# Another order for the first loads, sums on ScalarE for the first scales, and a planner that counts eight transfers in flight

## The chip, the cores and the metric

One core of a Trainium2 chip runs the kernel. The time is the device time of one execution in microseconds (us). The time before is 1918.88 us, the median of three runs (1918.65 to 1921.34).

## What is computed

Attention in chunks, then a mixture of eight experts whose weights are balanced over the tokens. For 4 batches of 768 tokens, 8 heads of 64 elements, chunks of 32 tokens that see 16 tokens to the left, 8 to the right and 8 memory keys:

```python
k_full = np.concatenate([mem_k, k_ctx], axis=2)
v_full = np.concatenate([mem_v, v_ctx], axis=2)
scores = scale * np.matmul(q_c, k_full.transpose(0, 1, 3, 2))
a = np.exp(scores - np.max(scores, axis=-1, keepdims=True))
a = a / (np.sum(a, axis=-1, keepdims=True) + 1e-09)
out[:, :, c_start:c_end] = np.matmul(a, v_full)
...
P = np.exp(logits)              # logits = x @ w_gate, x [3072, 512]
for _ in range(8):
    P /= P.sum(1, keepdims=True) + 1e-09
    P /= P.sum(0, keepdims=True) + 1e-09
    P *= N / E
for e in range(E):              # 8 experts, 512 -> 1024 -> 512
    h = np.maximum(x @ w1[e], 0.0)
    out += P[:, e:e + 1] * (h @ w2[e])
```

## The kernel before, in words

The 3072 tokens are six units of 512. A unit is four attention blocks of 128 tokens, numbered 0 to 23 over the whole run. For one block TensorE (PE) turns queries and keys (`tq`, `tk`, and `tx` for the keys beyond the block and the memory keys), multiplies them (`sp`), turns the shares (`ta`), multiplies by the values (`xp`) and turns the result (`xt`) into the transposed tokens `xg`. ScalarE (ACT) empties most of these banks, DVE takes the row maxima and divides.

The experts' products run in float16, with each operand as a high and a low part: ACT writes `high = scale * value`, DVE writes `low = scale * value - high` (`split`, L508). Each product has three passes. The scale is a power of two from the largest absolute value in a tensor: `most` (L558, DVE) reduces each quarter of an expert's weights, 128 x 1024, to one column of `mxs`; `scales` (from L434) then goes over the partitions by a transposition (`row_w`), a maximum, two bit operations, a broadcast by matmul (`sp_w`) and a reciprocal (`sw`). The values' maxima (`vmax`, L974) give the token scale `sx` in the same way; that one is used as soon as the values of two blocks are there.

The first expert of the first unit is done plainly (`first_hidden`, products `pp`, L2045; outputs `yp`, L2126), every later product by a seven-product scheme. `pp` of quarter 0 needs the split of `w1f` quarter 0, with the scale over all four quarters, and the split of the first 256 tokens, thus blocks 0 and 1 complete. Until then PE runs fill matmuls on the identity (`warm`, L427).

All order comes from `Plan` (L91): every step is added with an engine, a cost in us, its dependencies and a due time (`prio`); `Plan.run` plays the steps once, when the kernel is built, and lets each engine take the ready step with the least due time. The instructions of an engine then stand in that order, and on the chip each engine works through them strictly in order. DMAs are steps of the engine that issues them (SP, or ACT for some of the first): `dma` is the time that the transfer is believed to take in one common stream, and a transfer is believed to be usable 2.6 us after its part of the stream. Real DMAs take one of eight semaphores in turn, and an issue waits until the DMA that had this semaphore eight issues ago has landed. The due times of the first loads are in `BLOCKS`, `VALUES` and `FIRST` (L732 to L734).

The first loads are 256-byte rows of queries, keys and values (`q`, `k`, `kx`; values as one DMA for each of the four chunks and each parity of heads, 56 KB apiece, into `v_pair`), then `w1f` in two DMAs per quarter with rows of 512 bytes, then blocks 2 and 3, then `w2f` with rows of 2048 bytes. Half of the values of blocks 0 and 1 and the memory values are issued on ACT's queue, where the copies of the memory rows (`copy_m0`, L908) follow. Operands that are needed again are stored (`xkeep`, 1792 KB per unit), accumulators too (`akeep`, 256 KB).

## Time and profile before

| what | us |
|---|---|
| median of three runs | 1918.88 |
| lowest, highest run | 1918.65, 1921.34 |
| the profiled execution | 1919.81 |
| its span, first to last instruction | 1917.9 |
| PE busy in the span | 1903.2 |
| DVE, ACT, GpSimd busy | 1436.4, 1033.6, 524.4 |

The span is what the trace covers; the profiled execution's time is 1.9 us more than it, and 0.9 us above the median of the runs. A PE that counts as busy may be running fill matmuls, so its busy time alone doesn't tell how much of the span is needed work.

### The profile page before, as it was taken

How to read it: one execution, taken by the hardware profiler on the slowest of the kernel's cores; microseconds unless marked ns; L12 is line 12 of the kernel's file. 1: busy time of each engine (PE TensorE's matmuls, PEld its weight loads, DVE VectorE, ACT ScalarE, POOL GpSimd, SP SyncE). 2: the span in 40 equal slices, each digit the busy share in tenths (PEclk: the TensorE clock that was granted, in tenths of full speed). 3: DMA queues.
4: the chain of work that ended last, by engine and by line, in shares of the span. 5: the costliest groups of instructions: out<-in, count | busy, mean ns of one | idle time of the engine just before them, and what ended most of it. 6: DMA issues, size and time to landing. Idle time of an engine off the chain costs nothing.

```text
span 1917.9 us, 47295 instructions
## 1 busy us (share of the span) xinstructions
PE 1903.2 (99%) x19616; PEld 1641.0 (86%) x19616; DVE 1436.4 (75%) x2396; ACT 1033.6 (54%) x2019; POOL 524.4 (27%) x549
## 2 busy tenths in 40 slices
PE   9999999999999999999999999999999999999999
PEld 7777676688888888888888888888888888888888
DVE  6776569778679866898668875898678885786565
ACT  4765565556456545646445554655555554564453
POOL 1220001544224221432124231342124232332112
PEclk9999999999999999999999999999999999999999
DMA  8678753453235342265214533245313732322321
GB/s 198 174 194 209 171 172 116 129 204 125 83 110 172 127 148 85 78 197 185 92 63 149 197 105 127 78 160 176 138 45 105 242 122 94 100 83 84 127 83 67
DMA packets 246791, 254.82 MB, mean 133 GB/s; under 512 B 113264, under 2 KB 180272, under 8 KB 242224
## 3 DMA queue, kind: packets, MB, share of 16 engines
q1 hardware_dynamic: 244452, 251.21, 41.2%
q8 instruction: 153, 2.51, 0.6%
q10 hardware_dynamic: 2124, 0.59, 0.2%
q14 instruction: 62, 0.51, 0.1%
HBM read 187.84 MB, written 63.44 MB: 131 GB/s over the span
## 4 chain that ended last, share of the span: by engine, by line
PE 96%; DMA 2%; DVE 1%; ACT 0%; issue 0%; SPq 0%; ACTq 0%; DVEq 0%
PE px L1598 26%; PE yx L1598 23%; PE pz L1598 13%; PE yz L1598 11%; PE py L1598 6%; PE yp L2126 6%; PE yy L1598 6%; DMA q<-in_q_dram 1%; PE xp L1137 1%; PE sp L1069 1%; PE pp L2045 1%; PE tq L1006 1%; PE tk L1010 0%; PE ta L1127 0%; PE xt L1178 0%; DVE w L521 0%
## 5 line engine op out<-in xcount | busy, mean ns | idle before, releaser
L1598 PEld LDWEIGHTS <-w 128*128 128x128 f16 x7896 | 771.4, 98 | 91.9 <-issue 0.6
L1598 PEld LDWEIGHTS <-h 128*128 128x128 f16 x7056 | 690.4, 98 | 81.4 <-issue 1.5
L1598 PE MATMUL px<-x,w 128*128 128x256 f16 x4512 | 549.1, 273 | 0.0
L1931 POOL TENSOR_TENSOR acc<-acc,y 128x256 f32<-128x256 f32 x252 | 267.5, 1068 | 862.1 <-ACT y L1906 842.7
L1598 PE MATMUL yx<-w,h 128*128 128x256 f16 x4032 | 467.5, 273 | 1.3 <-DVE acc L1941 1.3
L1657 ACT ACTIVATE q<-px 128x256 f32<-128x256 f32 x376 | 142.8, 381 | 294.2 <-PE px L1598 289.5
L1598 PE MATMUL pz<-x,w 128*128 128x256 f16 x2256 | 278.2, 273 | 0.0
L1598 PE MATMUL yz<-w,h 128*128 128x256 f16 x2016 | 233.8, 273 | 0.0
L1826 DVE TENSOR_TENSOR h<-ss,h 128x1024 f16<-128x1024 f32 x160 | 215.0, 1346 | 4.0 <-ACT h L1802 3.5
L1777 ACT ACTIVATE h<-c 128x768 f16<-128x768 f32 x168 | 140.8, 838 | 106.4 <-DVE c L1667 106.4
L1802 ACT CAST h<-ss 128x1024 f16<-128x1024 f32 x168 | 174.1, 1039 | 20.4 <-DVE ss L1766 19.6
L1766 DVE SCALAR_TENSOR_TENSOR ss<-c,ss 128x256 f32<-128x256 f32 x336 | 168.3, 501 | 8.2
L1810 DVE SCALAR_TENSOR_TENSOR h<-c,h 128x768 f16<-128x768 f32 x168 | 165.3, 984 | 9.2 <-ACT h L1777 9.1
L1667 DVE SCALAR_TENSOR_TENSOR c<-px,q 128x256 f32<-128x256 f32 x188 | 78.0, 422 | 103.2 <-PE px L1598 94.9
L1906 ACT ACTIVATE y<-yx,pscale 128x256 f32<-128x256 f32 x168 | 79.4, 473 | 114.8 <-PE yx L1598 110.6
L1598 PE MATMUL py<-x,w 128*128 128x256 f16 x1128 | 139.2, 273 | 0.0
L2126 PE MATMUL yp<-w,h 128*128 128x512 f16 x576 | 132.0, 379 | 0.0
L1667 DVE SCALAR_TENSOR_TENSOR c<-py,q 128x256 f32<-128x256 f32 x188 | 78.5, 422 | 60.2 <-PE py L1598 56.7
L1766 DVE SCALAR_TENSOR_TENSOR ss<-c,h 128x512 f32<-128x512 f32 x168 | 120.8, 719 | 3.1 <-ACT h L1754 3.0
L1598 PE MATMUL yy<-w,h 128*128 128x256 f16 x1008 | 116.9, 273 | 0.0
L2126 PEld LDWEIGHTS <-h 128*128 128x128 f16 x576 | 56.0, 98 | 57.9
L513 ACT ACTIVATE w<-ws,sw 128x1024 f16<-128x1024 f32 (+1 forms) x64 | 69.3, 1089 | 65.5 <-POOL ws L602 65.5
(158 smaller groups left out, 1773.0 us busy)
## 6 DMA issues: line engine op xcount, KB each, us to landing
x<-xkeep SPq DMA_DIRECT2D x28, 1792.0 KB
akeep<-acc SPq DMA_DIRECT2D x168, 256.0 KB
acc<-akeep SPq DMA_DIRECT2D x168, 256.0 KB
w1f<-in_moe_w_dram SPq DMA_DIRECT2D x72, 256.0 KB
w2f<-in_moe_w_dram SPq DMA_DIRECT2D x32, 512.0 KB
w1fm<-in_moe_w_dram SPq DMA_DIRECT2D x56, 256.0 KB
w2fm<-in_moe_w_dram SPq DMA_DIRECT2D x28, 512.0 KB
xkeep<-x SPq DMA_DIRECT2D x6, 1792.0 KB
```

The source lines that it names most:

```text
L513: lambda: nc.scalar.activation(dst(0), src(), AF.Copy, scale=s),
L1598: nc.tensor.matmul(dst.t, a, b, start=(not more and n == 0), stop=(n == end), skip_group_check=more,)
L1657: lambda: nc.scalar.activation(t.t, src.t, AF.Copy, scale=DOWN),
L1667: lambda: nc.vector.scalar_tensor_tensor(c.t[:, o], src.t, DOWN, q.t, op0=ALU.mult, op1=ALU.add),
L1766: lambda: nc.vector.scalar_tensor_tensor(dst(), src(), 0.0, other(), op0=ALU.max, op1=op),
L1777: lambda: nc.scalar.activation(h.t[:, 0, 0:3], c.t, AF.Relu),
L1802: lambda: nc.scalar.copy(h.t[:, 0, 3:7], ss.t),
L1810: lambda: nc.vector.scalar_tensor_tensor(h.t[:, 1, 0:3].rearrange("p a n -> p (a n)"), c.t.rearrange("p a n -> p (a n)"), 0.0, h.t[:, 0, 0 ...
L1826: lambda: spare.tensor_tensor(h.t[:, 1, 3:7], ss.t, h.t[:, 0, 3:7], op=ALU.subtract),
L1906: (lambda: nc.scalar.activation(t.t, src.t, AF.Copy, scale=f))
L1931: lambda: nc.gpsimd.tensor_tensor(acc.t[:, cols], acc.t[:, cols], q.t, op=ALU.add),
L2126: nc.tensor.matmul(py.t, hf.t[:, hl, where[fh], o : o + P], room(fp, WIDE * wl + DM * fh, WIDE * wl + DM * (fh + 1)), start=(fp == 0 and i ...
```

## The change

The planner's model of DMAs is replaced: eight lanes (`LANES`), each transfer starts when a lane is free, at 0.45 us per issue, moves in one common stream, and gives its lane back 1.2 us after its part of the stream. Many costs of transfers are smaller (`xkeep` 4.3 instead of 7.0, `akeep` 0.7 instead of 1.3, queries and keys 1.25 instead of 1.55). ACT's activation table is loaded by a first small activation. The values, and the copies of the memory rows, all go to SP's queue, the copies behind the first half of block 0's values. A quarter of `w1` comes in one DMA with rows of 1024 bytes, and the four quarters stand between the halves of block 1's values. Rows in front of a batch's first token, and behind its last, are no longer loaded. The scales of the first expert's weights come from sums of absolute values, made by ACT (`total`), with two more bits of `SHIFT`, instead of DVE's maxima. The value maximum of block 1 is placed behind its scores, those of blocks 2 and 3 behind the split of `w1` quarter 1. Where the layout of `w1`'s tiles changes, the reading side (`tile1`, `tokens`, `cut`) follows it.

```diff
-ISSUE = 0.5
+ISSUE = 0.45
+LANES = 8
+VWORK = 1.1
+WORK2 = 1.8
+BEFORE = 0.7
+TABLE = 2.2
+COLD = 4.5
 BEHIND = 5.0
-FIRST = 2.0
+SHARE = 1.5
+BEGIN = 1.0
+AFTER = 1.2
+LATER = 1.0
 MARGIN = 8.0
-APART = 3.6
+APART = 2.5
...
             if t.dma:
-                at = max(at, dma - BEHIND)
-                t.start = at
-                clock[t.eng] = at + t.cost
-                dma = max(dma, at + t.cost / 2) + t.dma
-                t.end = max(dma, at + t.cost) + 2.6
+                if self.fill is None:
+                    at = max(at, dma - BEHIND)
+                t.start = max(at, lanes[0])
+                for _ in range(t.count):
+                    at = max(at, lanes.pop(0))
+                    work = t.dma / t.count
+                    if self.fill is None:
+                        work *= SHARE
+                    dma = max(dma, at + BEGIN) + work
+                    lanes.append(dma + AFTER)
+                    at += ISSUE
+                clock[t.eng] = at
+                t.end = dma + AFTER
...
-                    late = MARGIN if s.prio - t.end > FAR else 0.0
+                    late = MARGIN if s.prio - t.end > FAR else LATER if s.eng == "PE" else 0.0
...
+    first = misc.tile([P, 1], F32, name="first")
+    nc.scalar.activation(first, one, AF.Exp)
...
-            if which == 1:
-                for fh in range(2):
-                    queue.dma_start(st.t[:, fh], w1v[e, fp, :, :, fh])
+            if which == 1:
+                queue.dma_start(st.t.rearrange("p k a f -> p k (a f)"), w1v[e, fp])
...
+    def total(e, fp, which, st, deps, prio):
+        def go():
+            nc.scalar.activation(
+                room(0, 0, 1024),
+                st.t.rearrange("p k a f -> p (k a f)" if which == 1 else "p a d -> p (a d)"),
+                AF.Abs,
+                accum_out=mxs[:, e, which - 1, fp : fp + 1],
+            )
+
+        return add("ACT", 1.2, go, deps, prio, [st, first2[0]])
...
-    BLOCKS = (-50.0, -44.0, -30.0, -26.0)
-    VALUES = (-47.0, -41.0, -28.0, -24.0)
-    FIRST = (-38.0, -20.0)
+    BLOCKS = (-50.0, -49.0, -30.0, -26.0)
+    VALUES = (-47.0, -44.0, -28.0, -24.0)
+    FIRST = ((-45.5, -43.5, -42.5, -41.5), (-20.0, -19.5, -19.0, -18.5))
...
-                add(eng, parts, lambda i=i, on=on: go_v((i,), on), lv, at, [vt], dma=1.35)
-                for i, (eng, on) in enumerate(
-                    (("SP", nc.sync), ("ACT", nc.scalar) if n < 2 else ("SP", nc.sync))
-                )
+                add("SP", parts, lambda i=i: go_v((i,), nc.sync), lv, at + i, [vt], dma=VWORK)
+                for i in range(2)
...
-                dma=7.0,
+                dma=4.3,
...
-            found.append(most(0, fp, which, st, [ld], at - 12.0))
-        scale_w(0, which, found, at - 10.0, "att")
+            found.append(total(0, fp, which, st, [ld], at - 12.0))
+        scale_w(0, which, found, at - 10.0, "att", SHIFT + 2)
```

How the instructions stand. The line numbers of the changed kernel are about 25 to 60 higher for the same step.

SP's queue, from block 0's values to block 2's queries; `q_1`, `k_1` are queries and keys of block 1, `w1f_0_2` is quarter 2 of the first expert's `w1`. Before:

```order
L921 DMA v_pair_159<-in_v_dram 16x4x64
L921 DMA v_pair_159<-in_v_dram 40x4x64
L921 DMA v_pair_159<-in_v_dram 56x4x64 x3
L848 DMA q_1_188<-in_q_dram 128x8x64
L845 DMA k_1_192<-in_k_dram 128x8x64
L790 DMA kx_0_175<-in_k_dram 32x8x64 x2
L921 DMA v_pair_159<-in_v_dram 56x4x64 x4
L549 DMA w1f_0_0_286<-in_moe_w1_dram 128x4x128 x2
L549 DMA w1f_0_1_334<-in_moe_w1_dram 128x4x128 x2
L549 DMA w1f_0_2_341<-in_moe_w1_dram 128x4x128 x2
L549 DMA w1f_0_3_376<-in_moe_w1_dram 128x4x128 x2
L848 DMA q_2_432<-in_q_dram 128x8x64
```

The same place of the queue now:

```order
L973 DMA v_pair_161<-in_v_dram 40x4x64
L973 DMA v_pair_161<-in_v_dram 56x4x64 x3
L956 DMA v_pair_161<-v_pair_161 8x7x260 x2
L973 DMA v_pair_161<-in_v_dram 40x4x64
L973 DMA v_pair_161<-in_v_dram 56x4x64 x3
L573 DMA w1f_0_0_293<-in_moe_w1_dram 128x4x256
L973 DMA v_pair_161<-in_v_dram 56x4x64 x4
L573 DMA w1f_0_1_318<-in_moe_w1_dram 128x4x256
L973 DMA v_pair_161<-in_v_dram 56x4x64 x4
L573 DMA w1f_0_2_413<-in_moe_w1_dram 128x4x256
L573 DMA w1f_0_3_418<-in_moe_w1_dram 128x4x256
L893 DMA q_2_426<-in_q_dram 128x8x64
```

The keys and queries of block 1 now stand ahead of all values, both halves of each block's values are on this queue, and four single DMAs of `w1` stand where eight stood behind everything.

ACT, from block 0's result to the first split of weights; `xg` is the transposed result, `s_1` the shares of block 1, `x_0` the token operand. Before:

```order
L1184 COPY xg_0_478<-xt_0_470 128x4x128
L1108 ACTIVATE s_1_483<-s_1_483 128x512
L1146 COPY at_1_517<-ta_1_511 128x512
L1184 COPY xg_0_478<-xt_1_589 128x4x128
L1034 ACTIVATE qT_2_619<-tq_2_609 128x512
L513 ACTIVATE x_0_626<-xg_0_478,sx_110 128x512 x2
L1014 COPY kC_158<-tk_2_631 128x4x3x56
L513 ACTIVATE w1_0_0_650<-w1f_0_0_286,sw_112 128x1024
```

The same place now:

```order
L594 ACTIVATE w2_0_0_374,mxs_117<-w1f_0_1_318 128x1024
L1242 COPY xg_0_460<-xt_0_445 128x4x128
L1204 COPY at_1_463<-ta_1_454 128x512
L594 ACTIVATE w2_0_0_374,mxs_117<-w1f_0_2_413 128x1024
L594 ACTIVATE w2_0_0_374,mxs_117<-w1f_0_3_418 128x1024
L1242 COPY xg_0_460<-xt_1_530 128x4x128
L538 ACTIVATE x_0_550<-xg_0_460,sx_112 128x512 x2
L1088 ACTIVATE qT_2_567<-tq_2_552 128x512
L538 ACTIVATE w1_0_0_584<-w1f_0_0_293,sw_114 128x1024
```

The sums (L594) stand in ACT's order ahead of the copy of block 1's result; that of quarter 0 stands just before these rows, and `s_1` between it and the first of them. On DVE the four maxima are gone, and the splits of three quarters now stand ahead of the value maximum of block 2.

SP's queue around the first store of token operands, `xkeep_0`; `q_8`, `k_8` belong to block 8. Before:

```order
L549 DMA w1f_0_0_1408<-in_moe_w1_dram 128x4x128 x2
L2150 DMA akeep_0_134<-acc_0_0_1398 128x512
L549 DMA w1f_0_1_1423<-in_moe_w1_dram 128x4x128 x2
L1256 DMA xkeep_0_116<-x_0_626 128x7168
L848 DMA q_8_1463<-in_q_dram 128x8x64
L845 DMA k_8_1564<-in_k_dram 128x8x64
L790 DMA kx_2_1589<-in_k_dram 32x8x64 x3
```

Now:

```order
L573 DMA w1f_0_0_1287<-in_moe_w1_dram 128x4x256
L573 DMA w1f_0_1_1325<-in_moe_w1_dram 128x4x256
L2208 DMA akeep_0_136<-acc_0_0_1289 128x512
L893 DMA q_8_1337<-in_q_dram 128x8x64
L1314 DMA xkeep_0_118<-x_0_550 128x7168
L890 DMA k_8_1345<-in_k_dram 128x8x64
L836 DMA kx_2_1353<-in_k_dram 32x8x64 x3
```

`q_8` has moved ahead of the store, `k_8` is still behind it. From `q_2` to this place the queue holds 83 issues instead of 89. Over the whole program PE has the same products in number and size; of the fill matmuls 93 are left of 168, and 87 instead of 157 stand ahead of the first `pp`.

## Rows read from the trace of the kernel before

**Rows 1.** Windows by stage: us, then busy us of each engine (instructions), clock, DMA share, GB/s.

```profile
core 0: us, PE busy (x) PEld busy (x) DVE busy (x) ACT busy (x) POOL busy (x), PEclk, DMA share, GB/s
0.00:33.91 33.91, 29.95 (x469) 24.31 (x470) 17.27 (x36) 14.62 (x26) 4.95 (x12) 1.00 0.82 182
33.91:120.00 86.09, 82.80 (x1560) 62.37 (x1561) 65.83 (x114) 61.67 (x123) 21.54 (x26) 1.00 0.76 194
120.00:300.00 180.00, 177.07 (x3035) 127.90 (x3013) 115.36 (x228) 103.24 (x211) 17.07 (x21) 1.00 0.67 175
460.00:1900.00 1440.00, 1440.00 (x13193) 1290.63 (x13191) 1103.39 (x1782) 764.87 (x1492) 407.62 (x423) 1.00 0.36 122
```

**Rows 2.** The same view for the fill matmuls (tile warm) alone.

```profile
0.00:33.91 33.91, 20.71 (x157) 1.00 0.82 182
```

**Rows 3.** Waits of PE from 33.9 to 300: who for whom, total us, times, longest.

```profile
PE xp L1137 <- issue: 2.5, 2, 1.7
PE tq L1006 <- DMA q<-in_q_dram: 2.4, 3, 1.1
```

**Rows 4.** Timeline, PE and its weight loads (PEld), where real products begin.

```profile
33.38 1.14 PE L2045 MATMUL pp<-x,w 128*128 128x256 f16 x6
33.91 0.33 PEld L2045 LDWEIGHTS <-w 128*128 128x128 f16 x4 [0.42 <-DVE w L521]
```

**Rows 5.** Timeline, DVE, 25 to 34.

```profile
26.36 1.21 DVE L558 TENSOR_REDUCE mxs<-w1f 128x1 f32<-128x1024 f32 x1
28.04 0.13 DVE L445 TENSOR_REDUCE most_of<-mxs 128x1 f32<-128x4 f32 x1
30.70 0.16 DVE L457 RECIPROCAL sw<-uw 128x1 f32<-128x1 f32 x1
31.44 1.22 DVE L974 TENSOR_REDUCE vmax<-w 128x1 f32<-128x1024 f32 x1
32.58 3.67 DVE L521 SCALAR_TENSOR_TENSOR w<-w1f,sw,w 128x1024 f16<-128x1024 f32 x3
```

**Rows 6.** Timeline, ACT, 27 to 34.

```profile
27.19 0.59 ACT L1184 COPY xg<-xt 128x512 f32<-128x512 f32 x1 [3.39 <-PE xt L1178]
29.09 1.33 ACT L513 ACTIVATE x<-xg,sx 128x512 f16<-128x512 f32 x2 [0.42 <-DVE sx L457]
30.93 3.23 ACT L513 ACTIVATE w<-w1f,sw 128x1024 f16<-128x1024 f32 x3
```

**Rows 7.** Timeline, ACT and its queue, the first 11 us.

```profile
1.67 5.77 ACTq L921 DMA_DIRECT2D v_pair<-in_v_dram  x9
9.14 1.28 ACT L1034 ACT_TABLE_LOAD   x1 [9.14 <-DMA v_pair<-in_v_dram]
10.44 0.60 ACT L1034 ACTIVATE qT<-tq 128x512 f32<-128x512 f32 x1
```

**Rows 8.** DMA view, 0 to 40: moved GB/s in each us.

```profile
GB/s 0 15 207 158 237 165 148 121 94 57 145 136 200 270 214 128 75 218 308 301 259 299 339 321 291 259 154 35 127 117 118 204 272 204 138 146 117 281 373 360
```

**Rows 9.** DMA totals: 18 to 25 (w1), 27 to 32 (values), 38.3 to 43.4 (w2).

```profile
DMA packets 4655, 2.12 MB, mean 302 GB/s; under 512 B 976, under 2 KB 4654, under 8 KB 4654
DMA packets 2440, 0.60 MB, mean 120 GB/s; under 512 B 2440, under 2 KB 2440, under 8 KB 2440
DMA packets 1990, 1.85 MB, mean 363 GB/s; under 512 B 1238, under 2 KB 1238, under 8 KB 1988
```

**Rows 10.** Timeline, SP's queue around the first store of token operands.

```profile
70.15 3.95 SPq L921 DMA_DIRECT2D v_pair<-in_v_dram  x8
78.32 0.60 SPq L1256 DMA_DIRECT2D xkeep<-x  x1
79.01 0.45 SPq L848 DMA_DIRECT2D q<-in_q_dram  x1
79.55 5.50 SPq L845 DMA_DIRECT2D k<-in_k_dram  x1
```

**Rows 11.** The chain that ended last, 40 to 130: the transfers that PE waited for.

```profile
79.01 10.05 DMA q<-in_q_dram
```

More of the change, by code (lines that the diff above doesn't have):

```diff
@@ L23 @@
 HSHIFT = 18
-ISSUE = 0.5
+ISSUE = 0.45
[5 more added lines that the diff above has]
+COLD = 4.5
 BEHIND = 5.0
-FIRST = 2.0
+SHARE = 1.5
+BEGIN = 1.0
+AFTER = 1.2
+LATER = 1.0
 MARGIN = 8.0
-APART = 3.6
+APART = 2.5
 FAR = 60.0
 class Task:
-    __slots__ = ("eng", "cost", "fn", "prio", "left", "ready", "end", "then", "takes", "frees", "n", "dma", "start", "many")
+    __slots__ = ("eng", "cost", "fn", "prio", "left", "ready", "end", "then", "takes", "frees", "n", "dma", "start", "many", "count")
 class Past:
@@ L110, in add @@
         t.many = many
+        t.count = cost
         if dma:
@@ L133, in pad @@
                     self.fill(bank, n)
-                    heappush(banks, (now + 0.11 * n + 0.2, bank))
+                    heappush(banks, (now + step * n + 0.2, bank))
                 return
@@ L164, in run @@
     def run(self):
-        clock = {e: 0.0 for e in self.ENGINES}
+        clock = dict.fromkeys(self.ENGINES, BEFORE)
+        clock["ACT"] = TABLE
         waiting = {e: [] for e in self.ENGINES}
         able = {e: [] for e in self.ENGINES}
-        dma = FIRST
+        dma = 0.0
+        lanes = [0.0] * LANES
         for t in self.tasks:
@@ L913, in take_m, with clear @@
             nc.gpsimd.tensor_copy(vt.t, vs[0][0].t)
+        def clear():
+            for par in range(2):
+                nc.gpsimd.memset(vt.t[par * KW : par * KW + LC, 0, :, 0:D], 0.0)
         def go_v(pars, queue):
@@ L931, in go_v @@
                         part(c, 0, S - CH - LC, CH + LC)
-                        part(c, CH + LC, S - RC, RC)
                     else:
@@ L938, in load_values @@
             fill_ones = add("POOL", 0.3, lambda: nc.gpsimd.memset(vt.t[:, :, :, D:DV], 1.0), (), at, [vt])
-        parts = CB + (first or last)
+        parts = CB + (n == EARLY - 1)
         if n < BU:
@@ L982, in load_values @@
         if n < BU:
-            at = START - 14.0 + n // 2 * 17.0
-            vfound.append(add("DVE", 1.21, most, lv, at, [vt]))
-            if n == BU // 2 - 1:
-                scale_x(NU, vmax[:, 0:2], vfound, START - 12.0)
-            elif n == BU - 1:
+            at = (5.0, 12.0, 33.0, 33.0)[n]
+            if n == 1:
+                second.append((most, lv, vt))
+            else:
+                behind = wo[0, 1, 1][1] if n > 1 else []
+                vfound.append(add("DVE", 1.21, most, lv + behind, at, [vt]))
+            if n == BU - 1:
                 scale_x(0, vmax[:, 0:BU], vfound, at + 2.0)
```

105 lines of the change are left out of this document (64 added, 41 removed).

## The prediction

> **What bounds the kernel now.** I read the windows by stage first. From 460 to 1900 PE is busy for all of 1440.00 us at full clock [rows 1]: there PE's products alone set the time, and the change leaves their number and size as they are. From 33.91 to 120 PE is idle for 86.09 - 82.80 = 3.3 us, from 120 to 300 for 2.9 us [rows 1]. The one large reserve is the first stage: up to 33.91 PE counts 29.95 us busy, but 20.71 of them are 157 fill matmuls [rows 1, 2]. So a first product that starts earlier takes its whole advance off the end, as long as nothing behind it gives the time back.
>
> Then what the first product waits for. The first six products of `pp` start at 33.38, and the weight loads for the next wait 0.42 us until 33.91 for DVE's split of `w1` [rows 4]. That split starts at 32.58, behind a value maximum of block 2 (31.44), which stands in the order ahead of it [rows 5]; ACT's half started at 30.93 [rows 6], when the scale `sw` was there (30.70 + 0.16) [rows 5]. The scale comes from a reduction at 28.04, and that from the last of four maxima, which DVE starts at 26.36 [rows 5]. The flow of transfers is at 259 to 339 GB/s up to 26 and falls to 154 and 35 in the next two us [rows 8]. I therefore put the landing of the last quarter of `w1` at 25.5, and the tail from there to 33.91 at 8.4 us.
>
> Why so late? From 6 to 13 us only 0.90 MB move (the seven values from 148 to 200 sum to 901), 129 GB/s, against a mean of 192 from 2 to 6 us (207, 158, 237, 165) [rows 8]. In that time ACT is held by nine issues for 5.77 us, so its table load begins at 9.14 and the first turned queries are taken at 10.44 [rows 7].
>
> **The change, part by part.** *Landing of `w1`.* The loads up to its last quarter are 4.4 MB (the sizes of the DMAs in the order: 1.3 MB of queries and keys, 0.9 MB of values, 0.1 MB of copies, 2.1 MB of `w1`). From below: 2.2 MB of 256-byte rows at the 192 GB/s of 2 to 6 us [rows 8] take 11.4 us, `w1` at 302 GB/s [rows 9] takes 6.9; with 2 us before the first byte that ends at 20.3, 5.2 us earlier than now. From above: nothing gained, if eight in flight and one queue hold the flow down as they do now. I take 21.3, 4.2 us earlier: the stretch at 129 GB/s goes if its 0.90 MB run at 192 (4.7 us instead of 7, so 2.3), `w1` between the values fills the stretch at 128 and 75 GB/s from 15 to 17 us [rows 8] (about 1), the dropped rows are worth 0.3, and wider rows in `w1` about 0.6: `w1` with 512-byte rows ran at 302 GB/s, `w2` with 2048-byte rows at 363 [rows 9], 2.1 MB at either is 6.9 or 5.8 us, and I take half of the difference.
>
> [...]
>
> *The tail.* DVE's four maxima go, 1.21 us each [rows 5]; ACT gets four sums. The trace of before has no activation with a sum; the nearest row is the split of the same 128 x 1024, 3.23 us for three, 1.08 each [rows 6]. I take 1.2, bounds 1.08 and 1.6. Three sums are done before the last quarter lands, so one counts. Behind it ACT has the copy of the result (0.59), two splits of tokens (1.33) [rows 6] and a turned query (0.60) [rows 7], 2.5 in all; the scale chain beside it took 28.04 to 30.86, 2.8 us, with a split of tokens among it [rows 5]. So ACT's split of quarter 0 starts 1.2 + 2.8 = 4.0 after the landing, lasts 1.1, and DVE's lasts 1.2 (3.67 for three) [rows 5], now without the maximum ahead of it: 6.3 us instead of 8.4, a gain of 2.1. PE's wait ends at 21.3 + 6.3 = 27.6 instead of 33.9, 6.3 us earlier. For this, block 1's result must be ready for its copy 1.2 us after the landing, at 22.5; now the copy starts at 27.19 [rows 6], so attention has to be 4.7 us sooner. Its first turned queries were taken at 10.44, behind ACT's nine issues and a table load from 9.14 to 10.42 [rows 7]. Both leave that place, and I expect the queries to be taken by 5.
>
> *The fill matmuls.* 157 become 87; they cost nothing, as PE waits there anyway. If the cover goes, PE idles instead.
>
> *Behind the start.* Four more sums on ACT for `w2` (4 x 1.2) stand between reads of `pp` banks; ACT is busy for 61.67 of 86.09 us there, DVE for 65.83 [rows 1], so the sums fit and DVE's chain becomes shorter by four maxima; I take 0 for it, bounds -1.6 (half of PE's idle 3.3) and +2. *The stores.* Now the planner believes in transfers that are faster: for a load behind `xkeep` it allowed 7.0 + 2.6 = 9.6 us, now 1.0 + 4.3 + 1.2 + 1.0 = 7.5 (the constants of the diff). Measured is 10.05 us for `q_8`, issued 0.69 us behind the store [rows 10, 11], and PE waited for queries 2.4 us in all, 1.1 at most [rows 3]. `q_8` now goes ahead of the store, `k_8` still behind it. SP's queue reaches the store earlier by 4.2 us and by 6 issues at 3.95 / 8 = 0.49 us [rows 10], at 78.3 - 7.1 = 71.2; `k_8` would land at 81 to 82. PE asked for block 8 at 79.0 + 10.05 - 1.1 = 88.0; 6.3 earlier is 81.7, and the changed order asks some products sooner. So it is a wait of 0 to 3.5 us there where 1.1 was. I take 1.0 us more for all stores together; bounds -1 and +12.6 (below). Narrower spacing of scores and other later orders: nothing, bounds -1 and +1.
>
> **The sum.** 4.2 + 2.1 - 1.0 = 5.3 us. The profiled execution took 1919.8, so 1914.5; it lies 0.9 above the median of the runs, so for a median 1913.6.
>
> **The rivals.** *The loads do not come sooner.* All values now go through one queue. While only values ran, 27 to 32, they made 120 GB/s [rows 9], and eight values took 3.95 us to issue [rows 10]. If the 0.9 MB of blocks 0 and 1 run at 120 instead of 192 to 210, they take 7.4 us instead of 4.4, and `w1` lands 3.0 later than I say, at 24.3: the gain is 1.2 + 2.1 - 1.0 = 2.3, the time 1916.6. For it: nothing but the issue of values limits that stretch. Against: `w1` now stands between them, whose 0.5 MB each keep the engines busy while four values are issued. [...]
>
> *ACT waits in order at a sum.* The sum of quarter 0 stands ahead of block 1's shares and both copies of results. If that quarter lands 2 us later than ACT comes to it, block 1 is through 2 us later and the tokens become the last to be ready: gain 3.3, time 1915.6. For it: ACT is not busy then. Against: the shares of block 1 also wait behind DVE.
>
> *More than the sum.* `w2`'s scale is ready sooner and DVE has 4.8 us less, so half of PE's idle 3.3 us behind the start goes, and `k_8` is in time: 6.3 + 1.6 = 7.9, time 1911.0. For it: DVE is the busiest engine there beside PE, 65.83 of 86.09 us [rows 1]. Against: ACT, which gets the work, also empties PE's banks.
>
> *Slower: the stores.* There are six `xkeep` stores. If behind each the allowance, 2.1 us shorter, shows as a wait of PE, that is 12.6 us; less the gain of 6.3 it is 6.3 slower, time 1925.2. It decides from 6.3 us of new waits on. For it: 10.05 us measured against 7.5 allowed. Against: with 9.6 allowed only 2.4 us of waits arose in all, and `q_8`, which waited longest, has moved ahead of its store.
>
> **How the numbers follow.** A change within 0.2%, 3.8 us (1915.0 to 1922.7), cannot be told from none. Forecast 0.49, loads not sooner 0.20, ACT in order 0.10, more 0.14, stores 0.07. Faster: the forecast, the larger gain and 0.04 of the ACT case, 0.67; within 0.2%: 0.20 + 0.06 = 0.26; slower 0.07. The range takes in the larger gain and a little beyond (landing at its lower bound) and the loads that come no sooner with 1.6 us of further waits: 1910.2 to 1918.2; the stores lie outside.
>
> **What would show it.** In the changed profile: no stretch under 150 GB/s between 6 and 13 us; the last sum (L594) starts at about 21.3 and lasts 1.2; the first split of weights on ACT 4 us later; the first `pp` at about 26.5 and its wait over at 27.6; 460 to 1900 unchanged. A last sum after 23.5 makes the landing wrong, a first `pp` more than 7 us behind it the tail; waits of PE on queries, keys or values over 3.5 us in total make the stores wrong, and a granted clock under 1.00 ahead of 34 would be a cost that I have left out.

## The result and the profile after

The changed kernel takes 1925.02 us (median of 14 runs, 1923.15 to 1926.68), the kernel before 1921.07 beside it (14 runs, 1918.29 to 1924.28). The ratio is 1.0021, with a 95% interval of 1.0012 to 1.0029: about 4 us slower, where I had forecast 5.3 faster. The profiled execution took 1923.93, with a span of 1922.1.

First the windows by stage of the changed kernel, cut where its first products begin (columns as in [rows 1]):

```profile
0.00:31.44 31.44, 24.55 (x399) 19.16 (x400) 11.99 (x31) 17.82 (x34) 6.04 (x15) 0.89 0.91 191
31.44:120.00 88.56, 81.85 (x1495) 60.49 (x1496) 61.69 (x108) 63.38 (x128) 21.34 (x26) 0.96 0.84 204
120.00:300.00 180.00, 177.52 (x3056) 129.31 (x3055) 117.62 (x233) 103.62 (x215) 16.89 (x21) 1.00 0.62 164
460.00:1900.00 1440.00, 1438.51 (x13172) 1288.58 (x13171) 1103.94 (x1783) 765.57 (x1491) 418.95 (x423) 1.00 0.36 122
```

The first stage ends 2.5 us earlier. But from there to 120 PE is now idle for 6.7 us instead of 3.3, its granted clock has a mean of 0.96, and even the stage from 460 on, which had no idle time, has 1.5 us.

The start, in the timeline (ACT, DVE and PE in order of time), answers to [rows 4 to 6]:

```profile
20.70 1.06 ACT L594 ACTIVATE w<-w1f 128x1024 f16<-128x1024 f32 x1 [3.22 <-DMA w1f<-in_moe_w_dram]
22.86 1.19 PE L1195 MATMUL xp<-v_pair,at 64*32 64x65 f32 x64 [2.76 <-ACT at L1204]
24.79 1.06 ACT L594 ACTIVATE w<-w1f 128x1024 f16<-128x1024 f32 x1 [0.41 <-DMA w1f<-in_moe_w_dram]
25.76 0.19 ACT L594 ACTIVATION_READ_ACCUMULATOR w<-w1f 128x1 f32 x1
28.71 0.17 DVE L482 RECIPROCAL sw<-uw 128x1 f32<-128x1 f32 x1
28.91 3.23 ACT L538 ACTIVATE w<-w1f,sw 128x1024 f16<-128x1024 f32 x3
30.64 0.38 PE L2103 MATMUL pp<-x,w 128*128 128x256 f16 x2
31.44 2.58 PE L2103 MATMUL pp<-x,w 128*128 128x256 f16 x22 [0.42 <-DVE w L546]
```

The last sum starts at 24.79, right behind the landing of its quarter (24.7). From the landing to the end of PE's wait it is 6.7 us, much as forecast (6.3); but the landing is 0.8 us earlier than my 25.5 for the kernel before, not 4.2.

Behind the start, PE's waits from 31.4 to 300 (columns as in [rows 3]), and PE's timeline around the longest:

```profile
PE tq L1060 <- DMA q<-in_q_dram: 3.1, 1, 3.1
PE pp L2103 <- issue: 1.7, 1, 1.7
PE xp L1195 <- issue: 1.4, 2, 1.2
```

```profile
49.83 0.83 PE L452 MATMUL warm<-ident 128*128 128x256 bf16 x6
53.78 1.08 PE L1060 MATMUL tq<-ident,q 128*128 128x128 f32 x4 [3.12 <-DMA q<-in_q_dram]
54.80 1.19 PE L1195 MATMUL xp<-w,at 64*32 64x65 f32 x64
55.92 1.11 PE L1064 MATMUL tk<-ident,k 128*128 128x128 f32 x4
56.83 2.76 PE L2184 MATMUL yp<-w,h 128*128 128x512 f16 x6
```

PE stands for 3.12 us at the turning of block 5's queries, with the values of block 3 (`xp`), keys and outputs (`yp`) queued behind it, and what follows runs at half speed: four transpositions take 1.08 us instead of 0.66. The windows view gives the granted clock (the value behind the engines, as a share of full speed; the next one, the busy share of the transfer engines, adds up the times of packets and passes 1 in the first of these rows, at 1.12): 0.50 from 18.94 to 25.77, where PE had idled for 1.92 us before it and 2.76 us within it, and a mean of 0.66 from 50 to 60.

```profile
18.94:25.77 6.83, 4.07 (x80) 2.81 (x78) 2.85 (x8) 4.24 (x8) 0.00 (x0) 0.50 1.12 254
50.00:60.00 10.00, 6.88 (x88) 4.42 (x87) 5.96 (x8) 4.93 (x6) 0.00 (x0) 0.66 0.93 158
```

In the kernel before the same ten us were full and at 1.00, and PE took these queries behind other products, after they had landed:

```profile
50.00:60.00 10.00, 9.88 (x184) 6.91 (x183) 8.44 (x18) 8.90 (x17) 2.90 (x3) 1.00 0.60 126
55.05 0.66 PE L1006 MATMUL tq<-ident,q 128*128 128x128 f32 x4
```

To see where the time goes I counted PE's needed work (every instruction but fill matmuls, at its usual duration) and took, at a time t of the kernel before, how much sooner another kernel has done the same work. This is worked out from the profiled executions. A value whose point lies beside a wait of PE depends on how it is read: at 60, 80, 100 and 240 it can shift by some 2 us (e6 at 100 by 3.5), at the other points by 0.3.

| lead over the kernel before, us, at | 34 | 50 | 60 | 80 | 100 | 240 | 300 | 460 | end |
|---|---|---|---|---|---|---|---|---|---|
| changed kernel | +2.5 | +3.7 | -2.5 | -3.2 | -3.9 | -1.3 | -2.9 | -2.0 | -4.3 |

So in this execution there are three losses of different kinds: 6.2 us from 50 to 60, some 3 us from 75 to 85 (the waits for "issue", at 80.3 and 86.7), and 2.3 us after 460. What comes back from 100 to 240 fits the kernel before's own waits (1.68 at 130, 1.00 at 177).

**The theory.** The planner places each step by the landing that it believes (by its own clock, which runs some 2 us ahead of the chip at 50). Printed from the planner of the changed kernel, the last quarter of `w1` is to land at 21.3 and block 5's queries at 47.4; measured are 24.7 and 53.7. The planner of the kernel before put those queries behind other work and their own landing (54.1) cost PE nothing there. So, says the theory, the new allowances, not the new order of loads, cost the time. Rivals: the fall of the clock is the main price; the queue that carries the copies, or ACT's order, holds the start down; the loss is paced by transfers whatever the order is.

### The profile page after: what moved, and what is told of

Same layout as the page of the kernel before. It is cut to its first block, busy times and chain, and to the rows that moved or that the text cites. A ratio compares the mean times of both kernels' runs of the same rounds, so it can differ in the third digit from the quotient of the medians.

```text
span 1922.1 us, 47021 instructions
## 1 busy us (share of the span) xinstructions
PE 1900.9 (99%) x19541; PEld 1636.7 (85%) x19541; DVE 1428.4 (74%) x2388; ACT 1042.1 (54%) x2036; POOL 532.8 (28%) x552
## 4 chain that ended last, share of the span: by engine, by line
PE 92%; DVE 4%; DMA 2%; SPq 1%; issue 1%; ACT 1%; DVEq 0%; ACTq 0%
PE px L1656 24%; PE yx L1656 23%; PE pz L1656 12%; PE yz L1656 11%; PE py L1656 6%; PE yy L1656 6%; PE yp L2184 6%; PE xp L1195 1%; PE pp L2103 1%; DVE ss L1824 1%; PE sp L1123 1%; DVE h L1868 1%; SPq L973 1%; DVE w L546 0%; PE xt L1236 0%
## 5 line engine op out<-in xcount | busy, mean ns | idle before, releaser
L1989 POOL TENSOR_TENSOR acc<-acc,y 128x256 f32<-128x256 f32 x252 | 277.1, 1107 | 865.6 <-ACT y L1964 852.9
L1884 DVE TENSOR_TENSOR h<-ss,h 128x1024 f16<-128x1024 f32 x160 | 207.1, 1296 | 3.7 <-ACT h L1860 3.7
L1824 DVE SCALAR_TENSOR_TENSOR ss<-c,ss 128x256 f32<-128x256 f32 x336 | 172.7, 514 | 8.2
```

The source lines that it names most:

```text
L1824: lambda: nc.vector.scalar_tensor_tensor(dst(), src(), 0.0, other(), op0=ALU.max, op1=op),
L1884: lambda: spare.tensor_tensor(h.t[:, 1, 3:7], ss.t, h.t[:, 0, 3:7], op=ALU.subtract),
L1989: lambda: nc.gpsimd.tensor_tensor(acc.t[:, cols], acc.t[:, cols], q.t, op=ALU.add),
```

## The experiments

Each lead row below is from that run's profiled execution; its median can differ from that execution by up to 3.5 us (e2 was profiled at 1921.03).

| run | median us | ratio to before, 95% interval | lead at 34 | 50 | 60 | 80 | 100 | 240 | 300 | 460 | end |
|---|---|---|---|---|---|---|---|---|---|---|---|
| e1 fills at block 5's queries | 1925.15 | 1.0030 (1.0019, 1.0041) | +2.6 | +3.7 | +0.6 | +0.6 | -2.7 | -0.3 | -2.7 | -2.3 | -4.5 |
| e2 transfers x 1.2 | 1917.49 | 0.9991 (0.9981, 1.0000) | +2.6 | +2.6 | +1.4 | +1.7 | -0.2 | -0.8 | -0.4 | +0.5 | -1.4 |
| e3 copies on ACT's queue | 1924.58 | 1.0023 (1.0014, 1.0031) | +2.7 | +3.4 | -2.4 | -2.8 | -2.8 | -1.1 | -3.2 | -2.4 | -4.6 |
| e4 maxima on DVE for w1 | 1923.37 | 1.0022 (1.0013, 1.0031) | +0.9 | +1.1 | -1.0 | -0.9 | -4.8 | -1.5 | -2.8 | -1.9 | -3.8 |
| e5 block 5 placed later | 1924.98 | 1.0018 (1.0009, 1.0027) | +3.5 | +4.6 | +0.1 | -0.2 | -0.5 | +0.6 | -0.9 | -0.2 | -2.3 |
| e6 spacing 3.6 | 1931.65 | 1.0058 (1.0045, 1.0070) | +3.1 | +3.5 | +1.6 | +1.6 | -4.9 | -2.6 | -9.2 | -8.5 | -10.4 |
| e7 x 1.2 and 3.6 | 1920.67 | 1.0006 (0.9997, 1.0015) | +2.4 | +3.4 | +1.5 | +1.4 | -1.9 | +1.1 | +0.5 | +0.4 | -1.5 |
| e8 block 5 and 3.6 | 1920.37 | 1.0006 (0.9997, 1.0015) | +1.7 | +1.9 | -0.7 | +0.2 | -5.0 | +0.2 | +0.5 | +1.3 | -0.7 |
| e9 old rule in the last part | 1925.07 | 1.0032 (1.0020, 1.0043) | +2.0 | +3.2 | -3.0 | -3.2 | -2.8 | -0.2 | -2.4 | -1.8 | -4.6 |
| e10 x 1.2, store 6.2 | 1918.31 | 0.9991 (0.9983, 1.0000) | +2.1 | +2.2 | +1.0 | +1.3 | +1.8 | +5.0 | +4.3 | +3.8 | +1.8 |
| e11 e9 and e10 | 1920.09 | 1.0006 (0.9997, 1.0015) | +3.1 | +4.3 | +2.7 | +2.2 | +1.8 | +5.4 | +4.3 | +2.1 | -0.4 |
| e12 narrow rows of w1 | 1925.39 | 1.0038 (1.0023, 1.0052) | +1.0 | +2.1 | -2.2 | -1.5 | -3.5 | -0.1 | -2.8 | -1.9 | -3.9 |
| e13 e10, last part 5.0 | 1915.34 | 0.9977 (0.9968, 0.9986) | +2.1 | +3.4 | +2.5 | +2.6 | +2.9 | +6.1 | +5.3 | +5.5 | +4.7 |
| e14 last part 5.0 alone | 1928.13 | 1.0037 (1.0024, 1.0051) | +1.7 | +2.9 | +0.9 | +1.0 | -4.2 | -2.9 | -5.0 | -8.7 | -9.0 |

**e1: is it the clock?**

```diff
         def go_q():
+            if n == 5:
+                room5 = tq.t.rearrange("p a b -> p (a b)")[:, 0:256]
+                for _ in range(28):
+                    nc.tensor.matmul(room5, idle[:, 0:P], idle, start=True, stop=True)
```

> The changed kernel with 28 fill matmuls (bf16, 256 columns) on PE ahead of the transposition of block 5's queries, in its own bank; nothing else moves. The changed kernel idles there for 3.12 us (50.66 to 53.78) and its granted clock is 0.50 from 53.08 to 59.90. Theory A (the fall of the clock is a price of its own, besides the wait): 28 fills of 0.109 us fill the wait, the clock stays at 1.00 to the end, block 5's queries are taken at the same time, and 3 to 3.4 us come back, about 1921.7 against 1925.0 for the changed kernel. Rival B (only the wait costs; what runs at half clock has slack behind it): the clock stays at 1.00 and the time stays within 1 us of the changed kernel.

The windows view from 50 to 60 shows the clock at 1.00 now:

```profile
50.00:60.00 10.00, 10.00 (x161) 7.09 (x159) 7.42 (x10) 7.64 (x12) 2.12 (x3) 1.00 0.87 157
```

The lead at 60 is +0.6 instead of -2.5: half speed after the wait did cost 3.1 us there. The end did not move. By 100 it is down to -2.7, 1.2 us better than the changed kernel, and at 300 the two are the same, since PE, earlier by 3 us, waits from 80 to 90 for the keys beyond block 8 (`tx`, 2.2) and for "issue" (1.2). So the mechanism was as theory A said, and the time as the rival said: time won ahead of the next late transfer is only waited out there.

**e2: believe the transfers 1.2 times as long.**

```diff
-                    if self.fill is None:
-                        work *= SHARE
+                    work *= SHARE if self.fill is None else 1.2
```

> The changed kernel, but the planner counts every early transfer with 1.2 times its time in the stream. It then believes the last quarter of w1 at 24.6 (measured in the changed kernel 24.7, believed there 21.3) and block 5's queries at 54.0 (measured 53.7, believed 47.4). Theory A (the loss comes from an order that rests on landings believed 3.5 to 6.3 us too early): PE takes block 5's queries behind other work, no wait of PE on queries over 1 us and no fall of the clock at 53, the first pp as in the changed kernel (30.6), so 6 to 6.5 us faster than the changed kernel, 1918 to 1919, 2 to 3 faster than the kernel before. Rival C (transfers are the bound up to 60 whatever the order; the lead of the start is lost there anyhow): 1921 to 1922, as the kernel before.

PE has no wait on queries from 50 to 60, the clock is 1.00 there and in the first 31 us, and the median is 1917.5, ratio 0.9991 against the changed kernel's 1.0021:

```profile
50.00:60.00 10.00, 10.00 (x179) 6.44 (x179) 8.33 (x12) 9.72 (x17) 4.36 (x5) 1.00 0.78 141
```

No transfer was changed, and SP's queue has the same order up to 73 us; behind that it differs too (`q_8` is behind the store again, as in the kernel before). So the order that rests on too early landings cost 5 to 6 us (PE's differs from 44 us on, SP's from 73). The first products come when they came before (wait over at 31.28, 31.44 in the changed kernel), so the half clock from 18.94 to 25.77 had cost nothing.

**e3 and e4: what holds the start?** The copies go back to ACT's queue (e3); DVE measures `w1` (e4).

```diff
-                nc.sync.dma_start(
+                nc.scalar.dma_start(
...
-            found.append(total(0, fp, which, st, [ld], at - 12.0))
-        scale_w(0, which, found, at - 10.0, "att", SHIFT + 2)
+            measure = most if which == 1 else total
+            found.append(measure(0, fp, which, st, [ld], at - 12.0))
+        scale_w(0, which, found, at - 10.0, "att", SHIFT + 2 * (which - 1))
```

> The changed kernel, but the two copies of memory rows (8 x 7 x 260 elements) are issued on ACT's queue again, not on SP's between the halves of block 0's values. Theory D (the copies on SP's queue and their landing of 3.6 us hold the values and w1 back): everything behind them is issued 1.6 us sooner, the last quarter of w1 lands at about 23 instead of 24.7, the first pp at about 29, the time at block 5's queries stays as it is, so 0 to 1.5 us faster than the changed kernel. Rival E (the copies' packets fill the transfer engines wherever they are issued): w1 lands at 24.4 to 24.9 as before, first pp within 0.5 us of 30.6.

> The changed kernel, but the four quarters of w1 are measured by DVE's maxima again (w2 keeps ACT's sums). Theory F (ACT standing in order at the sums delays block 1's product by 2.8 us at 20.1, but the last quarter lands so late that this costs nothing, and DVE has the longer tail): the wait of PE at 20.1 goes, the first pp comes 0.5 to 2 us later than 30.6. Rival G (ACT's order at the sums sets the first pp): first pp 1 to 2 us earlier. In both the time changes by less than 2 us, unless the place of block 5's queries changes.

In e3 the copies land 4.5 us earlier, at 8.0, and the last quarter of `w1` at 25.1, not at 23: nearer rival E. In e4 PE's wait for the copy at 20.1 goes (it now waits 2.2 us at 21.5 for a maximum), and the lead at 50 is 1.1 instead of 3.7: theory F, and the sums on ACT are worth 2.6 us there (the first `pp` comes at 35.3, behind scores that now stand ahead of it). At the end these 2.6 us are not seen: e4 has the ratio 1.0022, the changed kernel 1.0021. What holds `w1` is, by the busy shares (1.00 from 2 to 26 in the changed kernel), the transfer engines; no run changed how many transfers are in flight or which queue issues the values. Here are the windows of the kernel before from 2 to 26 and from 6 to 13 (the value ahead of GB/s is the mean busy share of the transfer engines):

```profile
2.00:26.00 24.00, 22.37 (x411) 18.26 (x409) 10.21 (x17) 8.61 (x18) 4.04 (x4) 1.00 0.91 206
6.00:13.00 7.00, 6.78 (x95) 5.76 (x93) 0.00 (x0) 3.41 (x7) 0.00 (x0) 1.00 0.63 129
```

and of the changed kernel:

```profile
2.00:26.00 24.00, 19.26 (x361) 15.08 (x360) 7.96 (x18) 11.62 (x27) 4.86 (x8) 0.86 1.00 211
6.00:13.00 7.00, 6.94 (x174) 5.43 (x173) 1.55 (x3) 4.81 (x13) 0.00 (x0) 1.00 0.80 139
```

Over the whole load the engines were busy for 0.91 of the time already, so by this measure 2.2 us of 24 were free. The change fills them to 1.00, but it moves only 211 instead of 206 GB/s: from 6 to 13 a packet of 256 bytes takes 23 ns in the mean where it took 19 (from the trace's packets; the median is 18 in both).

**e12: are wider rows worth anything?**

```diff
-                queue.dma_start(st.t.rearrange("p k a f -> p k (a f)"), w1v[e, fp])
+                if e == 0 and ahead == "":
+                    for i in range(2):
+                        queue.dma_start(st.t[:, :, i], w1v[e, fp, :, :, i * P : (i + 1) * P])
+                else:
+                    queue.dma_start(st.t.rearrange("p k a f -> p k (a f)"), w1v[e, fp])
```

> The changed kernel with each quarter of the first w1 in two DMAs with rows of 512 bytes, as in the kernel before, all else as it stands. Theory W (wider rows are worth what I put on them): the last quarter lands 0.6 us later than 24.7, at about 25.3. Rival (the transfer engines take as long per byte at 512 as at 1024, mean 28 against 57 to 60 ns a row): within 0.3 us of 24.7, but for the four further issues on SP's queue.

The last quarter lands at 26.3, 1.6 us later. 0.9 of that is there at the first issue of `w1` already (12.86 instead of 11.95), ahead of the edit; the last issue, behind four more, stands 3.4 us later in SP's queue (21.70 instead of 18.27). But the kernels with wide rows whose first issue of `w1` stood about as late (12.6 to 13.0 in e7 to e10, e13 and e14) landed at 25.0 to 25.8, so 0.5 to 1.3 us is left for the edit. The packet times don't decide either: a row of 512 bytes takes 28 ns in the kernel before and 31 in e12, one of 1024 in the changed kernel 59, which is the same per byte; but these are means, and the medians, 27, 27 and 48, favour the wide row by a tenth. The run can't separate the issues from the rows, so theory W stays open.

**e5: one step moved.** The planner is told that block 5's queries and keys are ready at 52.5 and 53.6.

```diff
         t = add("PE", 0.5, go_q, [lq], at, [qt, qT], takes=tq)
+        if n == 5:
+            t.ready = 52.5
```

> The changed kernel, but the planner takes block 5's queries and keys to be ready at 52.5 and 53.6 (it believed 47.4 and 48.7; its clock runs 2 us ahead of the chip there), so PE gets block 4's result, its turning and two outputs ahead of them; nothing else is set. Theory A (the place of that one step costs the wait of 3.1 and the clock): no wait on queries at 51, clock 1.00 from 50 to 60, PE's lead over the kernel before at 60 is +3 instead of -2.5. Then theory H (what is won at 60 is lost from 75 to 95, because PE's waits there for nothing the profile shows, 1.2 and 1.7 us in the changed kernel, end 1.2 to 1.6 us after a packet of its code that comes late behind the store of operands): the end is at most 1 us earlier than the changed kernel, 1923 to 1925. Rival A1 (nothing else is late): the 6 us stay, 1918 to 1919.

The wait for the queries goes, and another late transfer takes its place at once: PE waits 2.4 us for the gate's weights at 55.9, which the planner had also believed landed. The lead at 60 is +0.1. The median of 1924.98 is as theory H had it, and theory A has its wait but not its lead of +3; mending one place doesn't tell how much the others cost.

**e6, e7, e8: the waits for "issue".** Two of them in the changed kernel, in PE's timeline:

```profile
79.77 0.54 PE L1195 MATMUL xp<-x_room,at 64*32 64x65 f32 x34
81.48 0.46 PE L1195 MATMUL xp<-x_room,at 64*32 64x65 f32 x30 [1.17 <-issue]
...
86.27 0.38 PE L2103 MATMUL pp<-x,w 128*128 128x256 f16 x2
88.34 0.61 PE L2103 MATMUL pp<-x,w 128*128 128x256 f16 x4 [1.69 <-issue]
```

PE stops in the middle of a group, 34 of 64 matmuls done, and the profile shows nothing that it waits for. The profile's page lists a queue of the kind "instruction", q8, with 153 packets, and the trace gives each of them 16,384 bytes: one runs from 79.22 to 80.18, the next from 85.30 to 86.78. PE goes on 1.3 and 1.6 us after their ends. In the sixteen profiles together PE has 29 waits for "issue" of over 0.4 us, and every one ends 1.2 to 1.6 us after the end of such a packet. From this I take it that PE had run out of code, and I call them waits for code from here on. The 153 packets go with 39,082 matmuls and loads of weights, and how much code PE holds no run shows. The kernel before has two of these waits, 0.82 us at 45.3 and the 1.68 at 130. A group of 64 small matmuls, with its 64 loads of weights, is 128 instructions, in 0.86 us in the kernel before (`sp` at 12.64). The change had narrowed the spacing of such groups; the edit puts it back in the changed kernel (e6), in e2 (e7) and in e5 (e8).

```diff
-APART = 2.5
+APART = 3.6
```

> The changed kernel with the old spacing of the groups of 64 small matmuls (scores, values): 3.6 us of the planner's clock, not 2.5. Such a group is 128 instructions in 0.86 us. Theory H (PE outruns its code when such groups stand closer while a store fills the transfer engines): the waits for nothing shown from 75 to 90 (2.9 us in the changed kernel) go or fall under 1 us, the wait for block 5's queries stays, so 1.5 to 3 us faster than the changed kernel, 1921 to 1922.5. Rival I (the code comes late because of the store alone, at any spacing): those waits stay over 2 us and the time within 1 us of the changed kernel.

> Both: transfers counted with 1.2 times their time, and the spacing 3.6. With 1.2 alone PE waited for nothing shown 4.1 us from 34 to 300 (2.1 of it at 221.9, 0.8 at 86, 0.8 at 119) and the time was 1917.5. Theory H: those waits fall under 1.5 us, 2 to 3 us faster, about 1915. Rival I: they stay over 3 us, 1917 to 1918.

> The changed kernel with block 5's queries and keys ready at 52.5 and 53.6 for the planner, and the spacing 3.6. Theory A with H: the 6 us of the place and 1.5 to 3 of the code waits come back and stay, 1916 to 1918. Rival (the lead is paced by the stores and loads from 70 to 100, whatever PE's order): within 1.5 us of the changed kernel less the code waits, 1921 to 1923.

The waits for code fall as theory H said: from 2.9 to 0.9 (e6), from 4.1 to none that the waits view lists (e7), from 0.7 to 0.2 (e8). But the time doesn't follow: by the ratios e6 is 0.37% slower than the changed kernel and e7 0.15% slower than e2, where both were to be faster; e8 is 0.12% faster than e5, short of the 1916 to 1918. From 80 to 90 PE now waits for transfers behind the store of operands: these are PE's waits in e6, 34 to 300.

```profile
PE pz L1656 <- DVE c L1725: 5.0, 1, 5.0
PE tx L852 <- DMA kx<-in_k_dram: 4.3, 1, 4.3
```

In e7 it is 2.5 us on queries, in e8 4.2 on `kx`. (The 5.0 us of e6 at 259 are a place in DVE's order of their own.) In the changed kernel the store's packets start from 79.1 to 85.2 us, the loads of block 8's keys and those beyond it are issued from 76.3 to 83.9, and the two packets above start at 79.22 and 85.30, beside the store and just behind it. That whichever PE needs first shows the wait is read from these waits, and no run took the store away.

**e10: the store.**

```diff
-                dma=4.3,
+                dma=6.2,
```

(at both stores of operands, on top of the edit of e2)

> Transfers counted with 1.2 times their time, as in the 1917.5 us kernel, and the store of operands with 6.2 instead of 4.3 (so 7.4 in the stream, 9.6 with what follows, what the kernel before allowed). That kernel waited 0.8 for code and 0.7 for queries at 86 to 88, and 2.1 for code at 221.9, each behind such a store. Theory S (what stands behind the stores is planned too early): those waits fall under 1 us in all, 1.5 to 3 us faster, 1914.5 to 1916. Rival (the waits only move to another product): 1917 to 1918.5.

The waits of PE from 75 to 300 are now these, and no others; in e2 they were 4.1 for code and 0.9 for queries and keys:

```profile
PE sp L1122 <- issue: 0.5, 1, 0.5
PE tq L1059 <- DMA q<-in_q_dram: 0.4, 1, 0.4
PE pp L2102 <- issue: 0.2, 1, 0.2
PE xp L1194 <- issue: 0.2, 1, 0.2
```

Theory S is right on the waits, at the narrow spacing too, and the lead at 240 is +5.0, the best so far. Of the time nothing arrives that the runs can tell: 1918.3, the same ratio as e2, as the rival had it, and in the profile 3.2 us of the lead are lost from 240 on, 2.0 of them after 460.

**e9, e11, e13, e14: the 2 us after 460.** The changed kernel and e1 to e12 lose 1.9 to 2.8 us there. All of them that keep the new rule in the planner's last part show it as one wait of `px` at each of five expert boundaries; in the changed kernel (1.5 of its 2.3 us):

```profile
PE px L1656 <- DVE c L1725: 1.5, 5, 0.6
```

e9 and e11 bring the old rule for transfers back in the planner's last part, though with the new costs times 1.4, not the old costs; e13 and e14 keep the new rule and let a transfer be usable 5.0 us after its lane is free.

```diff
+            if t.dma and self.fill is None:
+                at = max(at, dma - BEHIND)
+                t.start = at
+                clock[t.eng] = at + t.count * 0.5
+                dma = max(dma, at + t.count * 0.25) + t.dma * 1.4
+                t.end = max(dma, at + t.count * 0.5) + 2.6
...
-                    t.end += LATER
+                    t.end += 5.0
```

(the first in e9 and e11, the second in e13 and e14)

> The changed kernel, but the planner's rule for transfers in its last part (weights and accumulators of the later experts) is the old one again: one stream, 0.5 us an issue, usable 2.6 us after its part. All before is as in the changed kernel. From 460 on the changed kernel loses 2.3 us to the kernel before: at each of five expert boundaries PE's px comes 0.46 us late, behind DVE's c. Theory J (that is a place in DVE's order which the new rule for transfers moves): the five waits go and the time is 2 us under the changed kernel, about 1922. Rival K (they come from the early part's order, or from what runs beside DVE there): they stay and the time stays at 1924.

> Both of the runs before in one: 1.2 times, the store with 6.2, and the old rule for transfers in the last part. Theories S and J together: 1912.5 to 1914, 5 to 7 us faster than the kernel before. Rivals K and that the waits only move: 1917 to 1918.5.

> The kernel with transfers counted 1.2 times and the store with 6.2 (1918.3 us; 5.2 us ahead of the kernel before at 280, 1.8 at the end), and in the last part each transfer is believed usable 5.0 instead of 1.0 us after its lane is free. In the planner's order DVE's split of a later expert's weights then stands behind c of the product before, as in the kernel before, not ahead of it; GpSimd's sums, which follow that split, no longer run beside the four operations of DVE that PE's px waits for (1.10, 1.48, 0.94 and 0.83 us there, 0.68, 0.95, 0.42 and 0.42 elsewhere). Theory L (the place of the split costs 0.4 us at each of five boundaries): no wait of px on c over 0.1 us after 600, about 2 us faster, 1916. Rival M (the boundary is late from PE's side, whatever DVE's order): the five waits of 0.23 stay, 1918.

> The changed kernel with that 5.0 alone. Theory L: the same waits go, 2 us faster than the changed kernel, 1922 to 1923, all of it after 600. Rival M: 1924 to 1925.

Theory J falls: four waits of 0.47 to 0.82 stay in e9, and e11 loses 2.5 us after 460. Theory L stands. In DVE's timeline of the changed kernel, one boundary:

```profile
836.46 1.27 DVE L546 SCALAR_TENSOR_TENSOR w<-ws,sw,w 128x1024 f16<-128x1024 f32 x1
837.65 0.42 DVE L1725 SCALAR_TENSOR_TENSOR c<-py,q 128x256 f32<-128x256 f32 x1
837.99 1.10 DVE L1824 SCALAR_TENSOR_TENSOR ss<-c,h 128x512 f32<-128x512 f32 x1
839.01 1.48 DVE L1868 SCALAR_TENSOR_TENSOR h<-c,h 128x768 f16<-128x768 f32 x1
840.41 1.80 DVE L1824 SCALAR_TENSOR_TENSOR ss<-c,ss 128x256 f32<-128x256 f32 x2
842.32 0.42 DVE L1725 SCALAR_TENSOR_TENSOR c<-py,q 128x256 f32<-128x256 f32 x1
```

and of e13, the same one:

```profile
829.25 0.41 DVE L1724 SCALAR_TENSOR_TENSOR c<-py,q 128x256 f32<-128x256 f32 x1
829.58 1.27 DVE L545 SCALAR_TENSOR_TENSOR w<-ws,sw,w 128x1024 f16<-128x1024 f32 x1
830.77 0.95 DVE L1867 SCALAR_TENSOR_TENSOR h<-c,h 128x768 f16<-128x768 f32 x1
831.64 0.87 DVE L1823 SCALAR_TENSOR_TENSOR ss<-c,ss 128x256 f32<-128x256 f32 x2
832.62 0.42 DVE L1724 SCALAR_TENSOR_TENSOR c<-py,q 128x256 f32<-128x256 f32 x1
```

The split `w` has moved behind `c`, as in the kernel before, and the chain from one `c<-py` to the next is 3.4 us long instead of 4.7. In the changed kernel GpSimd's sums ran from 837.81 on, beside the slow operations; in e13 GpSimd does nothing between 826.1 and 838.2:

```profile
838.19 3.02 POOL L1988 TENSOR_TENSOR acc<-acc,y 128x256 f32<-128x256 f32 x2 [12.07 <-ACT y L1963]
```

In the sixteen profiles, from 460 us on, the three forms (`h<-c,h`, `ss<-c,h`, `ss<-c,ss`) never take over 0.96, 0.69 and 0.43 us while GpSimd is idle, 6873 times in all; every slower one has GpSimd at work beside it, though not every one beside it is slower, and `c`, which reads a bank of PE, never is (0.41 to 0.43 us with GpSimd at work beside it or not, in the kernel before and the changed one). No run took the sums away alone. That the edit, with the place of the split, removes the waits is shown: e13 has no wait of PE on `c` after 460, and its windows are

```profile
31.77:120.00 88.23, 86.35 (x1650) 65.01 (x1652) 62.99 (x114) 67.25 (x135) 20.86 (x26) 1.00 0.83 207
120.00:300.00 180.00, 179.73 (x2982) 129.74 (x2970) 117.29 (x241) 104.46 (x213) 15.31 (x21) 1.00 0.62 167
460.00:1900.00 1440.00, 1440.00 (x13189) 1290.26 (x13188) 1097.44 (x1777) 761.13 (x1489) 399.19 (x422) 1.00 0.35 122
```

e13 beats both kernels: 1915.34 us, 0.23% under the kernel before (interval 0.14 to 0.32%), some 8 us under the changed one. e14 keeps all 460-to-end time too (-8.7 at 460, -9.0 at the end), yet it is slower than the changed kernel, not 2 us faster. Its orders are those of the changed kernel up to 311 us, so up to there it is a second execution of the same kernel. PE waited 1.6 us, not 3.1, for the queries at 51.5, and the clock stayed at 1.00:

```profile
50.00:60.00 10.00, 8.43 (x228) 5.45 (x216) 7.98 (x11) 8.77 (x16) 2.48 (x3) 1.00 0.92 164
```

Then it waited 1.6 for code and 3.1 for `kx` from 82 to 89. So the same order lost 6.2 us from 50 to 60 in one execution and 2.0 in the other, and both are some 4 us behind at 100: as in e1, most of what is saved at 50 is not seen behind the store. The 3.4 us that e14 loses from 400 to 460 fall where the edit has changed the order: a wait of 2.1 us of `yx` for ACT at 417.2, and the clock at 0.50 from 420.1 to 423.5. My expectation held in its place and failed in the sum.

**All runs together.** The five kernels whose early transfers count 1.2 times (e2, e7, e10, e11, e13) have ratios from 0.9977 to 1.0006, the changed kernel and the nine others from 1.0006 to 1.0058. So the believed landings decide, over many orders; which places in the order cost the 5 to 6 us no run tells, since mending one (e1, e5) didn't move the median.

## Why the prediction was wrong

- **What bounds the kernel.** Right for 460 to 1900 of the kernel before [rows 1], wrong in "460 to 1900 unchanged": DVE's order there depends on when the planner believes that weights land. The changed kernel loses 2.3 us from 460 on and e14 0.3, e10 2.0 and e13 0.8.
- **Landing of `w1`: the first failed step.** I took 21.3 (4.2 us gained); it landed at 24.7, 0.8 gained, and at 24.2 to 25.8 in the other kernels with these loads in wide rows. The step that failed is "the stretch at 129 GB/s goes if its 0.90 MB run at 192" and with it "`w1` between the values fills the stretch". I read GB/s [rows 8] as free capacity. The busy share says 0.91 from 2 to 26, 0.63 in the dip: by it at most 2.2 us could come, and the packets of 256 bytes took 23 ns in the mean instead of 19; the dip from 6 to 13 is at 139 GB/s now. "Wider rows in `w1` about 0.6" is neither shown nor refuted (e12). A row of 512 bytes took 28 to 31 ns in the mean and one of 1024 took 59, the same per byte; by the medians, 27 and 48, the wide row is a tenth faster. I had the 0.6 from two means with different neighbours [rows 9], and that comparison could not carry it. The rival of loads that do not come sooner had about the right landing (24.3) by luck: its reason, values issued on one queue, was tested by no run, and a busy share of 1.00 from 2 to 26 speaks against it.
- **The tail.** Right: 6.3 forecast, 6.7 measured; e4 puts the sums at 2.6 us, I had 2.1.
- **ACT in order at a sum.** It happened (PE waits 2.76 us at 20.1) and cost nothing that the runs show, since the last quarter was later still (e4).
- **The fills.** Fewer fills left PE idle before 17.63 (1.92 us) and 22.86 (2.76 us), and the granted clock was 0.50 from 18.94 to 25.77. That cost nothing at the start (e2).
- **"Narrower spacing of scores and other later orders: nothing, bounds -1 and +1": the step that turned the sign.** With the same edits and longer believed transfers the kernel is 5 to 6 us faster (e2). In the changed kernel it shows first as -6.2 from 50 to 60, a wait of 3.1 and 3.1 at half clock (e1); but taking either away left the end where it was (e1, e5), so it is the order as a whole that cost, not that place. I compared allowance with measurement for the stores alone. The kernel before's trace had the landing of block 5's queries at 54.1, and the new planner could be read to believe 47.4.
- **The stores.** I took +1.0, with `k_8` as the one that waits. The place was right and the size too small: about 3 us from 75 to 85. `k_8` was in time; PE's own code, keys beyond the block or queries waited, one or the other from kernel to kernel. The slower rival (six stores at 2.1 us, 1925.2) named the time almost to the digit by luck: the stores' share of it is 3 us, the rest is the queries, the boundaries and a start that gained less.
- **The sum.** Step by step in the changed kernel's profile: +2.5 at the start, +1.2 to 50, -6.2 to 60, +0.6 to 75, -3.1 to 85, +1.1 to 100, +2.6 to 240, -1.6 to 300, +0.9 to 460, -2.3 to the end, in all -4.3. Of the miss of 9.3 us (5.3 faster forecast, 4.0 slower measured) the landing is 3.4 and the order 5 to 6. That these add up is not shown term by term: e4 gave away 2.6 us of the start and ended no later. With longer believed landings (e13) the same loads and sums at the start give 4.3 us over the kernel before. That this lies near the 5.3 that I forecast is luck too: 3.4 of it are there at 50, the rest comes behind.

Open: what paces 240 to 460 in e1 and e14, where leads shrink through small waits on DVE and ACT; why the last part's old rule (e9) doesn't restore the old place of the split; and what wider rows are worth.

## What to carry to other kernels

Where a planner's costs change, print what it now believes for each transfer that the critical engine waits for and lay it beside the landings in the trace of before; here block 5's queries, believed to land 6.3 us too early, cost a wait of 3.12 us and 3.1 more at half clock, and a single one set right may only uncover the next (e5). Read a dip in GB/s together with the busy share of the transfer engines, since here small rows kept them busy at a lower rate: a row of 256 bytes took 19 to 23 ns in the mean, a packet of the store, 14,336 bytes, 535 (median), twice the bytes per ns or more. A lead is only worth what it still is behind the next late transfer, so count it stage by stage, as needed work done, before adding it up.
